# A gated long convolution and its gradients on one core: a 16-point factor on blocks of four channels, and half-partition spectral products in the backward stage

## The chip, the cores and the metric

The kernel runs on one core of one Trainium2 chip. The metric is the device time of one execution in microseconds (us). Four runs of the kernel before gave 566.2 to 569.9 us, with a median of 568.68 us. A second figure, the span in a profile, counts from the first to the last instruction of one profiled execution.

## The reference

Inputs are `A_q`, `A_k`, `A_v` (2048 tokens, 512 channels, bf16), a four-tap filter `shift_k`, a filter `ssm_k` of 2048 taps for each channel, a skip weight `ssm_D`, and the three weights of a gated layer of width 1376. The forward part, cut to what matters:

```python
xn = _layernorm(x)                      # x = A_q
kv = k_shift * v                        # k_shift: k through the four-tap filter
y  = irfft(rfft(pad(kv)) * rfft(pad(ssm_k)))[:, :S] + kv * ssm_D
s  = xn * y
g  = silu((sigmoid(xn @ w_gate) * (xn @ w_up)) @ w_down)
out = x + s * g
```

The kernel returns `out` and the gradients with respect to `A_q`, `A_k`, `A_v`, `shift_k`, `ssm_k`, `ssm_D` and the three weights: ten outputs. The backward part needs the convolution's transpose twice: the gradient `dy` in the spectral domain is multiplied by the conjugate spectrum of the filter (which gives the gradient of `kv`) and by the conjugate spectrum of `kv` (which gives the gradient of `ssm_k`).

## The kernel before

Channels are taken in four groups (`cg`) of 128. The long convolution is a transform of length 4096 made of three matrix steps on TensorE:

- `step1`: for each of 16 token residues `j`, two matmuls with the sine and cosine tables `Cf` (128 x 128 each). The result `Qg` has tokens' frequencies `k` on the partitions.
- `flip`: 32 transposes of 128 x 128 for each group, so that the residue `j` and a block of channels lie on the partitions and `k` lies along the free dimension (`Qf`). A block has eight channels: 16 x 8 = 128 partitions for the real part, and as many for the imaginary part in a second tile.
- `step3`: the factor of 16 points, as a block-diagonal matrix `BD`. A quarter group (`qq`) of 32 channels takes four matmuls of 512 columns (two for the real part, two for the imaginary part) into one PSUM tile of two banks, and one evacuation of 1024 columns.

Then `cmul` makes the product of two spectra on the vector engine (DVE): two operations of 1024 bf16 elements and two of 512. `inv3` is the inverse of `step3`: for each quarter group eight matmuls of 256 columns with the table `R`, and one evacuation. `inv1` is the inverse of `step1` with the tables `Ci`.

The program has three stages.

1. Forward spectral stage, from the start to about 160 us. Four streams of work are interleaved: the gated layer for ten token tiles (`strG`), the filter's spectra (`strK`: transposes of the filter, `step1`, `flip`), the data's spectra (`strV`: the four-tap filter on DVE, `step1`, `flip`), and `strX`, which runs `step3` on both, stores both spectra in DRAM (`KK_d`, lines 956 and 967), multiplies them and transforms back to `y2A`.
2. The gated layer's backward pass (`stepB`, with `z_gen`, `d_gen`, `x_gen`, and `f_gen` for the last tiles), from about 160 to 355 us.
3. Backward spectral stage, from about 360 us to the end: `frontC` runs `step1` and `flip` on the gradient, `backC` the rest for each group, and `dW` makes the three weight gradients (16 matmuls of up to 512 columns for each block), which depend on nothing in the other two streams. `backC` loads both stored spectra of a quarter group with one DMA (`ld_KK`, two buffers), makes two products of 32 channels with `cmul` (lines 1248 and 1249), and two inverses into `B1` and `B2`. At the end of a group come `inv1`, the pair `dks` and `dkv` on DVE, the filter gradient (32 matmuls), the four-tap gradient (16 matmuls and a reduction), and seven DVE operations of 2048 for the gradient of `k`.

No order is left to the hardware. Every operation is recorded (`Rec.add`) with its dependences, and a planner (`Rec.order`, line 337) simulates the five engines with estimated costs (`cost`, line 283, and `dcost`, line 312) and gives out operations in its order of time, on each engine the one that can start first and, among equals, the one recorded first. Each engine's queue then runs strictly in that order. The recorded order comes from `run_streams` (line 497), which interleaves streams by their share of work done. Evacuations of PSUM (`evac`) may go to the scalar engine (ACT) or to DVE; the planner takes DVE when ACT is late by more than a bound (line 404). DMAs are issued on the queue of GpSimd (POOL) or of SyncE (SP), each in order. PSUM tiles of the backward stage have two places of two banks each (`mm2c`), the weight gradients two places of their own (`acc`), and transposes two (`tr`). SBUF is one slab with rings of buffers; a ring's length says how many tiles may be in flight.

All recorded operations carry line 493 in the profile, the line that emits them.

Of the kernel before, what the change touches and what calls it, by code (L numbers as in the profile page):

```python
# [9 lines left out]
ALU = mybir.AluOpType  # L10
# [6 lines left out]
P = 128  # L17
# [20 lines left out]
FBS = [(0, 4), (4, 4), (8, 3)]  # L38

# [129 lines left out]
class Rec:  # L169
# [142 lines left out]
    def dcost(self, alt):  # L312
# [17 lines left out]
        rate = 360e3 if run >= 2048 else 300e3 if run >= 1024 else 250e3 if run >= 512 else 150e3 if run >= 256 else run * 500  # L330
# [6 lines left out]
    def order(self):  # L337
# [53 lines left out]
        while ndone < len(ops):  # L391
            best = None
            for e in self.ENGS:
# [7 lines left out]
                if either and e in ("scalar", "vector"):  # L401
                    o = min(either, key=lambda o: (max(o.ready, free[e]), o.n))
                    s = (max(o.ready, free[e]), o.n, e, 1)
                    late = free["scalar"] - s[0]
                    if e == "scalar" or late > (0.4 if c is None or c[0] > s[0] + 0.6 else 1.6):
                        if c is None or s[:2] < c[:2]:
                            c = s
# [115 lines left out]
def gen_fft_consts(nc, ar, a, b, negpi, Cf, BD, R):  # L523
# [10 lines left out]
    pa = tmp([1], i32)  # L534
    nc.vector.tensor_single_scalar(pa, pi_, 3, ALU.arith_shift_right)
    pe = tmp([1], i32)
    nc.vector.tensor_single_scalar(pe, pi_, 7, ALU.bitwise_and)
    paf = tmp([1], f32)
    nc.vector.tensor_copy(paf, pa)
    pef = tmp([1], f32)  # L540
    nc.vector.tensor_copy(pef, pe)
    cb = tmp([16, 8], f32)
    nc.gpsimd.iota(cb, pattern=[[1, 16], [0, 8]], base=0, channel_multiplier=0, allow_small_or_imprecise_dtypes=True)
    ce = tmp([16, 8], f32)
    nc.gpsimd.iota(ce, pattern=[[0, 16], [1, 8]], base=0, channel_multiplier=0, allow_small_or_imprecise_dtypes=True)
    ab = tmp([16, 8], i32)
    nc.vector.tensor_scalar(ab, cb, paf[:, 0:1], None, ALU.mult)
    mask = tmp([16, 8], f32)
    nc.vector.tensor_scalar(mask, ce, pef[:, 0:1], None, ALU.is_equal)
    ang = tmp([3, 16, 8], i32)  # L550
    nc.vector.tensor_single_scalar(ang[:, 0], ab, 12, ALU.add)
    nc.vector.tensor_single_scalar(ang[:, 1], ab, 8, ALU.add)
    nc.vector.tensor_copy(ang[:, 2], ab)
    nc.vector.tensor_single_scalar(ang, ang, 15, ALU.bitwise_and)
    angf = tmp([3, 16, 8], f32)
# [11 lines left out]
    tri = tmp([3, 16, 8], f32)  # L567
    nc.scalar.activation(tri, angf, ACT.Sin, bias=negpi, scale=2 * math.pi / 16)
    nc.vector.tensor_tensor(tri, tri, mask[:, None, :, :].to_broadcast([P, 3, 16, 8]), ALU.mult)
    nc.vector.tensor_copy(BD, tri.rearrange("p t b e -> p t (b e)"))  # L570
    for c, ci, t in ((0, 0, 0), (0, 1, 1), (1, 0, 2), (1, 1, 0)):
        nc.vector.tensor_scalar(R[:, c, :, :, ci], tri[:, t], SCALE_INV, None, ALU.mult)
# [9 lines left out]
def kernel_impl(ctx, tc, A_q, A_k, A_v, A_shift_k, A_ssm_k, A_ssm_D, B_x, B_w_gate, B_w_up, B_w_down,  # L582
# [8 lines left out]
    KK_d = dram.tile([NG, 4, 2, P, 2, 512], bf16, name="KK_d")  # L591
# [24 lines left out]
    BD = Ring(ar, [3, 128]).ap  # L616
    R = Ring(ar, [2, 16, 8, 2]).ap
# [57 lines left out]
    def f_ln2(i):  # L675
        xj, st = T[i]["xq"], T[i]["st"]
        nc.vector.scalar_tensor_tensor(nmr_all[:, i:i + 1], st[:, 6:7], -1.0, rstd_all[:, i:i + 1], ALU.mult, ALU.mult)
        nc.scalar.activation(xnA[:, i, :], xj, ACT.Identity, bias=nmr_all[:, i:i + 1], scale=rstd_all[:, i:i + 1])
# [55 lines left out]
    QgK_r = Ring(ar, [2, GG, NJ, 8])  # L734
# [5 lines left out]
    QgV_r = Ring(ar, [2, GG, NJ, 8])  # L740
# [76 lines left out]
    QfK_r, QfV_r = Ring(ar, [2, GG, 128], n=2), Ring(ar, [2, GG, 128])  # L817
    KFg_r = Ring(ar, [2, GG, 128])
    Bg_r = Ring(ar, [NJ, GG, 8, 2])
    Xc_r = Ring(ar, [2, 512], n=2)  # L820
    Yc_r = Ring(ar, [2, 512], n=2)
    t2_r = Ring(ar, [2, 512], n=2)
# [10 lines left out]
    def step1(src, Qg):  # L833
        for jb in range(2):
            for c in range(2):
                ps = ps_mm([8, GW], name="ps_q")
                for jj in range(8):
                    j = jb * 8 + jj
                    nc.tensor.matmul(ps[:, jj, :], Cf[:, c, j, :], src(j), start=True, stop=True)
                nc.evac(Qg[:, c, :, jb * 8:(jb + 1) * 8, :].rearrange("p g j e -> p j g e"),  # L840
                         ps[:].rearrange("p j (g e) -> p j g e", e=8), 1024)
                yield 1024

    def flip(Qg, Qf):
        for gb in range(GG // 8):
            for c in range(2):
                pt = ps_tr([8, 128], name="ps_fl")
                for gi in range(8):
                    nc.tensor.transpose(pt[:, gi, :], Qg[:, c, gb * 8 + gi].rearrange("p j e -> p (j e)"), ident)
                nc.evac(Qf[:, c, gb * 8:(gb + 1) * 8, :], pt[:], 1024)  # L850
                yield 1024

    def step3(Qf, qq, dst):
        qre = Qf[:, 0, 4 * qq:4 * qq + 4, :].rearrange("p g k -> p (g k)")
        qim = Qf[:, 1, 4 * qq:4 * qq + 4, :].rearrange("p g k -> p (g k)")
        ps = ps_mm([2, 512], name="ps_x")
        nc.tensor.matmul(ps[:, 0], BD[:, 0, :], qre, start=True, stop=False)
        nc.tensor.matmul(ps[:, 0], BD[:, 1, :], qim, start=False, stop=True)
        nc.tensor.matmul(ps[:, 1], BD[:, 2, :], qre, start=True, stop=False)
        nc.tensor.matmul(ps[:, 1], BD[:, 0, :], qim, start=False, stop=True)  # L860
        nc.evac(dst, ps[:], 1024)
        yield 2048

    def cmul(X, K, out, conj):
        T1, T2 = out, t2_r.next()
        nc.vector.tensor_tensor(out=T1, in0=K, in1=X[:, 0:1, :].to_broadcast([P, 2, 512]), op=ALU.mult)
        nc.vector.tensor_tensor(out=T2, in0=K, in1=X[:, 1:2, :].to_broadcast([P, 2, 512]), op=ALU.mult)
        o0, o1 = (ALU.add, ALU.subtract) if conj else (ALU.subtract, ALU.add)
        nc.vector.tensor_tensor(out=out[:, 0, :], in0=T1[:, 0, :], in1=T2[:, 1, :], op=o0)
        nc.vector.tensor_tensor(out=out[:, 1, :], in0=T2[:, 0, :], in1=T1[:, 1, :], op=o1)  # L870

    def inv3(Y, qq, Bg):
        ps = ps_mm([4, NJ, 16], name="ps_b")
        for gg in range(4):
            for c in range(2):
                nc.tensor.matmul(ps[:, gg].rearrange("p j x -> p (j x)"), Y[:, c, gg * 128:(gg + 1) * 128],
                                 R[:, c].rearrange("p j e c -> p (j e c)"), start=(c == 0), stop=(c == 1))
        nc.evac(Bg[:, :, 4 * qq:4 * qq + 4].rearrange("p j g e c -> p g j (e c)"), ps[:], 1024)
        yield 2048

    def inv1(Bg, dst):
        Bv = Bg.rearrange("p j g e c -> p j (g e) c")
# [64 lines left out]
    def strX():  # L947
        yield from gen_ci()
        for cg in range(NG):
# [4 lines left out]
            for qq in range(4):  # L954
                yield from step3(QfK, qq, KFg[:, :, 4 * qq:4 * qq + 4, :].rearrange("p c g k -> p c (g k)"))
                nc.gpsimd.dma_start(KK_d[cg, qq, 0].rearrange("p c (g k) -> p c g k", k=128), KFg[:, :, 4 * qq:4 * qq + 4, :])
# [6 lines left out]
            for qq in range(5):  # L963
                if qq < 4:
                    Xc = Xc_r.next()
                    yield from step3(QfV, qq, Xc)
                    nc.gpsimd.dma_start(KK_d[cg, qq, 1], Xc)
                    ys[qq] = Yc_r.next()
                    cmul(Xc, KFg[:, :, 4 * qq:4 * qq + 4, :].rearrange("p c g k -> p c (g k)"), ys[qq], False)
                    if qq == 3:  # L970
                        flags.add(("s3V", cg))
                if qq > 0:
# [4 lines left out]
                 (strX(), 4 * 28672 + 4096, 0.2, 1.0)])  # L977
# [447 lines left out]
```

## Time and profile before

| | |
|---|---|
| median of four runs | 568.68 us |
| the profiled execution, its own time | 564.83 us |
| its span | 563.1 us |
| TensorE clock granted | 1.00 throughout |
| matmuls of 128 columns | 3652, 229.9 us busy |
| matmuls of 256 columns | 384, 52.1 us busy |
| matmuls of 512 columns | 1141, 272.1 us busy |
| ACT evacuations of 1024 columns from f32 | 154, mean 1032 ns |
| DVE tensor-tensor, 1024 bf16 elements | 96, mean 684 ns |
| DVE tensor-tensor, 512 bf16 elements | 320, mean 416 ns |
| DVE tensor-tensor, 2048 bf16 elements | 68, mean 1217 ns |
| loads of stored spectra (`KK_d`), POOL queue | 16 of 512 KB, 5.7 us to landing |

How to read it: matmuls are pipelined, so a row's busy time is the union of overlapping instructions, and an instruction's duration is longer than the distance to the next one. "idle before, releaser" says how long an engine stood still before a group and what ended the wait. The chain of waits follows back from the last instruction to what released it. Windows give the busy time of each engine in a stretch, so that a stage can be read alone.

### The profile page before, as it was taken

What the parts mean: (1) busy time and instruction counts of PE and PEld (TensorE: products, weight loads), DVE (VectorE), ACT (ScalarE), POOL (GpSimd) and SP (SyncE); (2) the same over time, 40 slices, a digit from 0 to 9 for tenths busy, and PEclk for the clock granted to TensorE, in tenths of its full rate; (3) what the DMA queues carried; (4) which work ended last, traced back from release to release, by engine and by line L of the source; (5) the groups of instructions that cost most, each with busy time, mean ns of one, the idle gap of its engine ahead of it and who ended that gap; (6) DMA issues with size and microseconds to landing.
All of it is one profiled execution on the core that took longest, in us unless ns stands there. A gap on an engine that the chain in (4) does not pass through costs nothing.

```text
span 563.1 us, 13136 instructions
## 1 busy us (share of the span) xinstructions
PE 536.4 (95%) x5330; PEld 378.5 (67%) x5389; DVE 420.9 (75%) x873; ACT 342.9 (61%) x454; POOL 156.5 (28%) x266
## 2 busy tenths in 40 slices
PE   3999889999989999999999999999999999999996
PEld 2889678898768566776666765656756666565643
DVE  7589899947777998989898999437378487397350
ACT  7989999977986234444344543467758576345421
POOL 3135225303312321312231212313322522331212
PEclk9999999999999999999999999999999999999999
DMA  8899978675522999979979999998487598575433
GB/s 245 239 255 245 308 215 252 215 188 177 173 77 74 214 241 219 278 201 193 238 199 246 247 217 287 291 264 231 139 259 229 177 323 237 160 229 186 152 118 110
DMA packets 127367, 120.34 MB, mean 214 GB/s; under 512 B 74995, under 2 KB 107593, under 8 KB 127306
## 3 DMA queue, kind: packets, MB, share of 16 engines
q1 hardware_dynamic: 109722, 62.84, 46.4%
q0 software_dynamic: 17056, 56.66, 32.4%
q8 instruction: 42, 0.69, 0.5%
q14 instruction: 19, 0.16, 0.1%
q10 hardware_dynamic: 528, 0.00, 0.0%
HBM read 54.23 MB, written 47.55 MB: 181 GB/s over the span
## 4 chain that ended last, share of the span: by engine, by line
PE 72%; issue 9%; ACT 8%; DVE 7%; POOL 2%; DMA 1%; POOLq 0%; ACTq 0%; DVEq 0%
PE psum L493 72%; ACT slab L493 8%; DVE slab L493 7%; POOL out_dram L493 1%; DMA KK_d<-slab 1%; POOL slab L493 0%; POOL KK_d L493 0%; POOLq L1420 0%; POOL ksh_d L493 0%; POOLq L493 0%; ACTq L493 0%; DVEq L493 0%; POOLq L1409 0%
## 5 line engine op out<-in xcount | busy, mean ns | idle before, releaser
L493 PE MATMUL psum<-slab 128*128 128x128 bf16 (+4 forms) x5330 | 536.4, 261 | 21.3 <-ACT slab L493 13.0
L493 PEld LDWEIGHTS <-slab 128*128 128x128 bf16 (+1 forms) x5389 | 378.5, 99 | 178.8 <-issue 13.3
L493 DVE TENSOR_TENSOR slab<-slab 128x512 bf16<-128x512 bf16 (+3 forms) x555 | 291.5, 579 | 37.6 <-ACT slab L493 27.4
L493 ACT CAST slab<-psum 128x1024 bf16<-128x1024 f32 (+3 forms) x242 | 200.1, 857 | 99.3 <-PE psum L493 93.8
L493 ACT COPY slab<-psum 128x1024 bf16<-128x1024 bf16 (+2 forms) x94 | 79.4, 887 | 86.9 <-PE psum L493 86.3
L493 POOL DMA_DIRECT2D out_dram<-slab x75 | 44.6, 596 | 158.7 <-ACT slab L493 83.8
L493 DVE TENSOR_TENSOR slab<-psum,slab 128x512 bf16<-128x512 f32 (+2 forms) x68 | 44.3, 652 | 33.7 <-PE psum L493 24.9
L493 ACT ACTIVATE slab<-slab 128x512 bf16<-128x512 bf16 (+3 forms) x51 | 41.2, 809 | 18.3 <-DVE slab L493 17.9
L493 ACT ACTIVATE slab<-psum 128x512 bf16<-128x512 f32 (+1 forms) x64 | 37.7, 589 | 9.5 <-PE psum L493 8.0
L493 DVE SCALAR_TENSOR_TENSOR slab<-slab 128x1 f32<-128x1 f32 (+3 forms) x64 | 28.0, 437 | 13.8 <-ACT slab L493 12.6
L493 POOL DMA_DIRECT2D KK_d<-slab x32 | 20.0, 628 | 63.3 <-ACT slab L493 54.0
L493 DVE COPY slab<-psum 128x1024 bf16<-128x1024 bf16 (+2 forms) x22 | 14.0, 646 | 20.2 <-PE psum L493 18.7
L493 POOL DMA_DIRECT2D slab<-in_A_q_dram x29 | 16.3, 562 | 39.7 <-DMA out_dram<-slab 31.3
L493 DVE CAST slab<-psum 128x1024 bf16<-128x1024 f32 (+1 forms) x15 | 17.4, 1160 | 9.4 <-PE psum L493 9.2
L493 POOL DMA_DIRECT2D slab<-KK_d x16 | 11.6, 727 | 25.2 <-DVE slab L493 25.1
L493 DVE TENSOR_SCALAR slab<-slab 128x1 f32<-128x1 f32 (+8 forms) x49 | 16.7, 359 | 2.0 <-ACT slab L493 1.8
L493 POOL TENSOR_TENSOR slab<-slab 128x1 f32<-128x1 f32 x16 | 12.7, 796 | 18.7 <-DVE slab L493 18.5
L493 DVE SCALAR_TENSOR_TENSOR slab<-psum,slab 128x512 f32<-128x512 f32 x16 | 10.9, 684 | 6.7 <-PE psum L493 6.7
L493 POOL DMA_DIRECT2D slab<-in_grad_out_dram x16 | 8.7, 541 | 22.1 <-DMA out_dram<-slab 15.4
L493 POOL DMA_DIRECT2D slab<-slab x8 | 4.5, 567 | 26.6 <-issue 17.3
L493 DVE BATCH_NORM_STATS2 slab<-slab 128x6 f32<-128x512 bf16 x16 | 10.8, 683 | 0.0
L493 POOL DMA_DIRECT2D slab<-in_A_k_dram x12 | 10.1, 844 | 2.2 <-PE psum L493 1.7
(22 smaller groups left out, 44.4 us busy)
## 6 DMA issues: line engine op xcount, KB each, us to landing
KK_d<-slab POOLq DMA_DIRECT2D x32, 256.0 KB, 3.3
slab<-KK_d POOLq DMA_DIRECT2D x16, 512.0 KB, 5.7
out_dram<-slab POOLq DMA_DIRECT2D x58, 128.0 KB, 4.2
hS_d<-slab SPq DMA_DIRECT2D x16, 352.0 KB, 3.0
dgS_d<-slab SPq DMA_DIRECT2D x16, 352.0 KB, 5.0
duS_d<-slab SPq DMA_DIRECT2D x16, 352.0 KB, 4.8
slab<-hS_d SPq DMA_DIRECT2D x8, 512.0 KB, 5.0
slab<-dgS_d SPq DMA_DIRECT2D x8, 512.0 KB, 5.7
```

The lines of the kernel that those rows point to most:

```text
L493: getattr(getattr(self.nc, eng), meth)(*[place(v) for v in a], **{x: place(v) for x, v in k.items()})
```

## The change

A block has four channels instead of eight, and the real and imaginary parts share one tile: partition index = part (2) x residue (16) x channel (4). The constants have nine sections, each a (offset, factor) pair of angles, where the factor depends on the half of the partitions.

- `step3` takes a table index. One result of 1024 columns (a quarter group of 32 channels, both parts) takes two matmuls of 512 columns. `X_RI` gives (real, imaginary) in the two halves, `X_IR` the two exchanged, `X_IN` (imaginary, minus real).
- The filter's spectrum takes `X_RI` alone. The data's spectrum in the forward stage takes `X_RI` and `X_IR`, each with an evacuation of its own.
- The forward product is two full operations of 1024 and no sum: the sum over the parts is made by `inv3`, with two terms (`R_A`, `R_B`), 16 matmuls of 128 columns for a quarter group.
- In the backward stage `step3` makes `Xr` (`X_RI`) and `Xi` (`X_IN`). Each of the two products is four operations of 1024 on 64 partitions, two of which write the half that they don't read, and one full sum. `K` is overwritten. `inv3` then has one term (`R_W`), 8 matmuls of 128 columns for each product.
- Stored spectra are laid out so that a quarter group is 2 x 1024 for each partition. Their load goes to the SP queue, with four buffers and three quarters ahead instead of two. `Qf` has one buffer instead of two; `frontC` waits for the group before, between `step1` and `flip`.
- The layer norm's last step may go to ACT or DVE. The planner's DMA rates and its rule for evacuations change.

```diff
+GQ = GW // 4
+HALF = (0, 1)
+SECS = [(12, -4), (0, 12), (4, -4), (12, -8), (8, -8), (0, 0), (12, 0), (12, 4), (8, 4)]
+BDSEC = [(0, 1), (1, 0), (1, 2)]
+RSEC = [(3, 4), (5, 6), (7, 8)]
...
-        rate = 360e3 if run >= 2048 else 300e3 if run >= 1024 else 250e3 if run >= 512 else 150e3 if run >= 256 else run * 500
+        rate = 340e3 if run >= 2048 else 290e3 if run >= 1024 else 250e3 if run >= 512 else 150e3 if run >= 256 else run * 500
...
-                    late = free["scalar"] - s[0]
-                    if e == "scalar" or late > (0.4 if c is None or c[0] > s[0] + 0.6 else 1.6):
+                    late = free["scalar"] + self.cost(o.alts[0])[0] - s[0] - self.cost(o.alts[1])[0]
+                    if e == "scalar" or late > (0.3 if c is None or c[0] > s[0] + 0.6 else 1.5):
...
+    for n, (off, d) in enumerate(SECS):
+        if d:
+            nc.vector.tensor_scalar(ang[:, n], ab, dc[d][:, 0:1], float(off), ALU.add, ALU.add)
+        else:
+            nc.vector.tensor_single_scalar(ang[:, n], ab, float(off), ALU.add)
...
-        nc.scalar.activation(xnA[:, i, :], xj, ACT.Identity, bias=nmr_all[:, i:i + 1], scale=rstd_all[:, i:i + 1])
+        nc.add([("scalar", "activation", (xnA[:, i, :], xj, ACT.Identity), dict(bias=b, scale=r)),
+                ("vector", "tensor_scalar", (xnA[:, i, :], xj, r, b, ALU.mult, ALU.add), {})])
...
-                    nc.tensor.transpose(pt[:, gi, :], Qg[:, c, gb * 8 + gi].rearrange("p j e -> p (j e)"), ident)
+                nc.tensor.transpose(pt[:, gi, :], Qg.rearrange("p c j e g -> p (c j e) g")[:, :, g], ident)
...
+    def step3(Qf, qq, which, dst):
         ps = ps_mm([2, 512], name="ps_x")
-        nc.tensor.matmul(ps[:, 0], BD[:, 0, :], qre, start=True, stop=False)
-        nc.tensor.matmul(ps[:, 0], BD[:, 1, :], qim, start=False, stop=True)
-        nc.tensor.matmul(ps[:, 1], BD[:, 2, :], qre, start=True, stop=False)
-        nc.tensor.matmul(ps[:, 1], BD[:, 0, :], qim, start=False, stop=True)
+        lhs = BD[:, which].rearrange("p c j e -> p (c j e)")
+        for h in range(2):
+            nc.tensor.matmul(ps[:, h], lhs, Qf[:, 8 * qq + 4 * h:8 * qq + 4 * h + 4, :].rearrange("p g k -> p (g k)"),
+                             start=True, stop=True)
...
+    def inv3(terms, qq, Bg):
+        ps = ps_mm([8, NJ, 8], name="ps_b")
+        for g in range(8):
+            for n, (Y, r) in enumerate(terms):
+                nc.tensor.matmul(ps[:, g].rearrange("p j x -> p (j x)"), Y[:, g * 128:(g + 1) * 128],
+                                 R[:, r].rearrange("p j e c -> p (j e c)"), start=(n == 0), stop=(n == len(terms) - 1))
...
+                    yield from step3(QfV, qq, X_RI, Xc)
+                    nc.gpsimd.dma_start(KK_d[cg, qq, :, 1], Xc)
+                    nc.vector.tensor_tensor(Y, Xc, KFg[:, qq], ALU.mult)
+                    yield from step3(QfV, qq, X_IR, Xs)
+                    nc.vector.tensor_tensor(Xs, Xs, KFg[:, qq], ALU.mult)
+                    ys[qq] = ((Y, R_A), (Xs, R_B))
...
-            nc.gpsimd.dma_start(KK, KK_d[n // 4, n % 4].rearrange("t p c x -> p t c x"))
+            nc.sync.dma_start(KK, KK_d[n // 4, n % 4])
...
-            while cg > 1 and ("s3C", cg - 2) not in flags:
-                yield 0
             Qg = Qg_r.next()
             yield from step1(lambda j: y2A[:, j, cg * GW:(cg + 1) * GW], Qg)
+            while cg > 0 and ("s3C", cg - 1) not in flags:
+                yield 0
...
-                    cmul(Xc, KK[:, 0], Y1, True)
-                    cmul(Xc, KK[:, 1], Y2, True)
+                    lo, hi = slice(0, 64), slice(64, P)
+                    for t in range(2):
+                        K, T2 = KK[:, t], ys[qq][1][:, t]
+                        if t in HALF:
+                            nc.vector.tensor_tensor(T2[lo], K[lo], Xr[lo], ALU.mult)
+                            nc.vector.tensor_tensor(T2[hi], K[lo], Xi[lo], ALU.mult)
+                            nc.vector.tensor_tensor(K[lo], K[hi], Xr[hi], ALU.mult)
+                            nc.vector.tensor_tensor(K[hi], K[hi], Xi[hi], ALU.mult)
+                            nc.vector.tensor_tensor(T2, T2, K, ALU.add)
...
-                    yield from inv3(Y1, qq - 1, B1)
-                    ld_KK(cg * 4 + qq + 1)
-                    yield from inv3(Y2, qq - 1, B2)
+                    for t, B in ((0, B1), (1, B2)):
+                        yield from inv3(((T2[:, t], R_W),), qq - 1, B)
+                    ld_KK(cg * 4 + qq + 3)
...
-    KK_r = Ring(ar, [2, 2, 512], n=2)
-    Qf_r = Ring(ar, [2, GG, 128], n=2)
+    KK_r = Ring(ar, [2, 1024], n=4)
+    Qf_r = Ring(ar, [GQ, 128])
...
+    Xr_r, Xi_r, T2_r = Ring(ar, [1024], n=2), Ring(ar, [1024], n=2), Ring(ar, [2, 1024], n=2)
```

## The prediction

> **What bounds the kernel now.** I read the page first: busy shares, then the 40 slices, then the windows by stage, then the vector engine's timeline in the last stage.
>
> ```profile
> PE 536.4 (95%) x5330; PEld 378.5 (67%) x5389; DVE 420.9 (75%) x873; ACT 342.9 (61%) x454; POOL 156.5 (28%) x266
> ...
> PE 72%; issue 9%; ACT 8%; DVE 7%; POOL 2%; DMA 1%; POOLq 0%; ACTq 0%; DVEq 0%
> ```
>
> TensorE is the bound on average, and 72% of the chain of waits lies on it. But the change touches two stages only, so the windows decide (columns: the stretch and its length, busy us of PE, PEld, DVE, ACT and POOL with instructions, granted clock, DMA share, GB/s):
>
> ```profile
> 20.00:60.00 40.00, 38.66 (x617) 35.63 (x618) 34.05 (x60) 36.01 (x49) 16.14 (x26) 1.00 0.90 239
> 60.00:100.00 40.00, 35.19 (x466) 29.61 (x468) 37.70 (x65) 38.44 (x49) 15.55 (x25) 1.00 0.88 253
> ...
> 200.00:240.00 40.00, 39.84 (x423) 27.96 (x425) 36.61 (x96) 18.90 (x33) 10.74 (x19) 1.00 1.02 241
> ...
> 400.00:440.00 40.00, 39.73 (x337) 26.62 (x340) 28.15 (x45) 27.64 (x31) 11.29 (x18) 1.00 0.69 218
> 440.00:480.00 40.00, 39.68 (x310) 24.99 (x314) 27.70 (x45) 25.86 (x29) 14.77 (x21) 1.00 0.74 230
> ```
>
> In the forward spectral stage (13 to about 160 us) TensorE, ACT and DVE are all near full. In the backward spectral stage (from about 366) TensorE never pauses, and DVE and ACT have 30% each to spare. The DVE timeline there:
>
> ```profile
> 376.47 7.71 DVE L493 TENSOR_TENSOR slab<-slab 128x1024 bf16<-128x1024 bf16 x16 [1.67 <-ACT slab L493]
> ...
> 402.88 2.48 DVE L493 TENSOR_TENSOR slab<-slab 128x2048 bf16<-128x2048 bf16 x2 [7.67 <-ACT slab L493]
> ...
> 514.98 3.96 DVE L493 TENSOR_TENSOR slab<-slab 128x1024 bf16<-128x1024 bf16 x8 [1.28 <-DMA slab<-KK_d]
> 525.42 2.48 DVE L493 TENSOR_TENSOR slab<-slab 128x2048 bf16<-128x2048 bf16 x2 [6.47 <-ACT slab L493]
> ...
> 537.96 7.50 DVE L493 TENSOR_TENSOR slab<-slab 128x2048 bf16<-128x2048 bf16 x6
> ```
>
> The first spectral products start at 376.5, the pair `dks`/`dkv` of the first channel group comes at 402.9 and that of the last at 525.4, so a group takes 40.9 us. The last product ends at 518.9 and the last DVE operation at 545.5: a tail of 26.5 us, mostly latency. The 1 MB store of `out_2` follows (7.5 us to landing by the list of DMA issues, about 9 with its issue), so this branch would end near 554.5; the weight gradients on TensorE end the kernel after it. The branch has some 9 us of slack.
>
> Rates. In the forms list a tensor-tensor of 1024 lasts 684 ns and one of 512 417. The 16 in 7.71 us are eight of each; the durations sum to 8.81, so neighbours overlap by 73 ns: start to start 0.611 and 0.344, and one complex product takes 1.93. One of 2048 takes 1.22. The last full weight-gradient blocks are evacuated at 541.35, 544.81 and 548.26: 3.46 us for 16 matmuls of 512 columns, 216 ns each, so 108 for 256 columns. A stretch of 176 matmuls in 10.13 us gives 57.6 ns for 128 columns.
>
> [...] The 64 existing filter transposes step by 32 bytes, yet the 3652 matmuls of 128 columns average 220 ns, latency included[...].
>
> **The change part by part.**
>
> *Start.* Nine sections of constants instead of three: some 4 more 128x1 operations at 0.14 us, 6 more angle operations at 0.2, larger masks, then more copies. About 2 us of DVE ahead of the first sine (7.28), more behind it. TensorE is half idle there (11.46 of 20 us). Between 0 and +2; I take +1.
>
> *Forward, TensorE.* Filter spectra: 16 quarter groups x 2 fewer matmuls of 512 = 32 x 0.216 = -6.9. The data spectra keep their 4. The inverse becomes 16 of 128 instead of 8 of 256: 16 x (0.92-0.86) = +0.9. Sum -6.0.
>
> *Forward, ACT and DVE.* 16 more evacuations, 1.03 each: +16.5. Products: 1.93 becomes 2 x 0.611, 16 times: -11. The normalisation of 13 tiles may go from ACT (0.86) to DVE (estimate 0.2 from the 1408-element tensor_scalar at 0.54): -8. Net about -3 over the two engines. ACT is 90 to 96% busy in 20 to 100, so TensorE's 6 us come off only in part: bounds -6 and +3, I take -3.5. Start and forward: -2.5. The stage between (160 to 355) keeps its work.
>
> *Flips.* 384 transposes read every 32nd element. Bounds: 0, or a doubled pace (50 ns, 19 us); I take 0.
>
> *Backward, TensorE.* step3 keeps 4 x 512. The inverses: 16 x 256 become 16 x 128 per quarter group: 16 x (1.73-0.92) = -13.0. The weight gradients come forward into that room.
>
> *Backward, ACT.* 16 more evacuations, 1.03: from 69% to about 79%. Hidden.
>
> *The planner.* Its transfer rates fall by 3 to 6%, and the choice of an evacuation's engine now compares finishing times, which favours DVE for bf16 tiles (0.69 there, 1.06 on ACT) and ACT for f32 ones (1.22, 1.03). In the backward stage DVE has 4 bf16 evacuations now; four more would cost it 2.8 us, four fewer give as much. I take 0.
>
> *Backward, DVE.* Per quarter group, two products at 1.93 (3.86) become 10 operations of 1024, eight on 64 partitions[...]. Below: 10 x 0.611 = 6.1. [...] I take the held order: four of five at 0.684, 6.7 us. A group then costs 26.8 for products and 12.4 for the rest (9 x 1.22, 2 x 0.69), 39.2 against 27.8 now. TensorE's 40.9 us per group shrinks by 3.3, and by more where fewer gradients are interleaved. So the spare 30% is gone, and DVE sets the group. From the first product: 4 x 39.2 - 12.4 (the last group's rest lies in the tail) = 144.4. Stage 200 to 240 has DVE at 91.5% busy while not the bound; as the bound I take 96%: 150.4. The tail loses a little, as fewer gradients stand between: 24. End: 376.5 - 2.5 + 150.4 + 24 + 9 = 557.4.
>
> *Waits and queues.* An inverse waiting for the sum holds TensorE's queue: step3 of the next quarter and gradients stand behind it. The gradients are the cover as long as the written order puts them before the wait; its estimate for 1024 elements (0.603 in `cost`) is right for back-to-back operations but 10 us short over 128 held ones, which is what TensorE may wait. The spectra's load moves from POOL to SP, two quarters earlier, into 4 buffers: 16 issues of 0.73 us leave POOL, and the DVE waits on that load (5.2 us) go. On SP they stand among gradient loads which wait for their buffer; three quarters ahead is some 20 us of cover. `Qf` has one buffer: the next flip waits for the group's last step3, covered by its remaining products.
>
> *Sum.* TensorE's branch: 563.1 - 2.5 - 13.0 = 547.6 plus up to 10. DVE's branch: 557.4. The later counts: -5.7. The profiled execution took 564.83 (span 563.1 and 1.7 around it), so 559.1; it lies 3.9 under the median shown, so 563.0.
>
> **Rivals.**
>
> 1. TensorE keeps all it saves. Half operations overlap: 160 x 0.611 + 37.2 = 135.0, at 96% 140.6, end 547.6, equal to TensorE's branch: -15.5, 553.2. For it: DVE's 30% idle now[...].
> 2. Slower: DVE overruns in the backward stage. It decides from 152.5 us of DVE work (0.72 us per operation at 96%), or from 9% idle at my price: 374 + 158.9 + 33 = 565.9. With 14% idle, as the 6 to 8 us gaps at the group ends suggest if next-group products don't fill them: 374 + 167.9 + 33 = 574.9, +11.8: 580.5. [...] For it: those gaps; against: the four load buffers and two of `T2` allow half a group ahead.
> 3. DVE's branch ends just where TensorE's does now, and ACT eats the forward gain: 568.
>
> **How the numbers follow.** Forecast 0.35, rival 1 0.24, rival 2 0.27, rival 3 0.14. Faster by over 0.5% (about what a measurement can tell from no change): 0.28 of the forecast and rival 1, 0.52. Slower: rival 2 and 0.04 of rival 3, 0.31. Same: the rest, 0.17. Range 551 to 579: the PE bound with some forward gain below, rival 2 with 13% idle above. Both signs hold much, so the forecast's own range: 558 to 567.
>
> **What would show it.** DVE in 400 to 480 at 37 us of 40 or more, where it now has 28, and half operations starting 0.68 us apart; TensorE's waits naming DVE, above 5 us in all, from 366 on; the last DVE operation within 10 us of the end; `dks` pairs 39 to 42 us apart. Forward: the stage ends 2 to 5 us earlier. Wrong if TensorE ends at full occupancy with DVE under 85% in the backward stage (rival 1), if half operations last about 1.2 us, or if flips pace above 60 ns.

## The result and the profile after

| | before | after |
|---|---|---|
| median of all runs, us | 569.26 (63 runs) | 570.87 (44 runs) |
| ratio, 95% interval | 1 | 1.0041 [1.0026, 1.0055] |
| span of the profiled execution, us | 563.1 | 569.7 |
| last matmul of the weight gradients ends, us | 557.7 | 565.3 |
| last DVE operation ends, us | 545.5 | 553.3 |

By the prediction's own sums (6.0 us forward, 13.0 backward) the change takes some 19 us of matmuls out of the kernel, and yet it is 0.4% slower: a small difference, but the interval leaves out 1. The forecast was 5.7 us faster. The profiled execution of the kernel before took 564.83 us, 4.4 less than its median, and that of the changed kernel 571.5, 0.6 more than its own, so the two traces lie 6.7 us apart where the medians lie 1.6 apart. The page of the changed kernel, first its busy times and then the chain of waits:

```profile
PE 527.9 (93%) x5426; PEld 373.4 (66%) x5485; DVE 466.4 (82%) x908; ACT 359.7 (63%) x469; POOL 140.2 (25%) x250
...
PEclk9999999999999999999999999999999999999699
...
PE 44%; DVE 28%; ACT 11%; issue 11%; DMA 4%; POOL 2%; POOLq 0%; DVEq 0%; ACTq 0%
```

The chain was 72% TensorE and 7% DVE; now it is 44% and 28%. One slice of the 40 (527 to 541 us) has a granted clock of 6 tenths; the profiled execution of the kernel before has none such. All 44 executions of the changed kernel have a mean clock of 0.990 to 0.994, so this is not a matter of the one that was profiled. The windows by stage say where TensorE's room opens (columns as before: PE, PEld, DVE, ACT, POOL, clock, DMA share, GB/s):

```profile
20.00:60.00 40.00, 37.38 (x598) 35.41 (x599) 33.76 (x59) 34.00 (x43) 13.29 (x23) 1.00 0.77 199
60.00:100.00 40.00, 35.34 (x498) 30.71 (x503) 36.41 (x59) 38.96 (x49) 14.26 (x26) 1.00 0.89 276
...
400.00:440.00 40.00, 38.99 (x325) 24.17 (x329) 33.19 (x46) 31.47 (x37) 8.88 (x15) 1.00 0.68 221
440.00:480.00 40.00, 39.07 (x322) 23.79 (x326) 37.55 (x55) 28.28 (x33) 10.62 (x16) 1.00 0.72 233
480.00:520.00 40.00, 36.00 (x267) 20.88 (x269) 39.03 (x50) 22.80 (x28) 11.01 (x19) 1.00 0.63 191
520.00:570.00 50.00, 39.24 (x255) 23.28 (x255) 23.87 (x33) 14.57 (x20) 9.28 (x15) 0.90 0.36 110
```

From 400 to 480 TensorE is at 39 of 40 (39.7 before), with DVE risen from 28 to 33 and 38. From 480 on DVE has no room left (39.03 of 40) and TensorE loses 4 us in one window, more in the next. The same window of the kernel before, and the stretch from 360 to 560 us, first before and then after:

```profile
480.00:520.00 40.00, 39.79 (x260) 23.51 (x262) 28.15 (x45) 16.95 (x21) 11.93 (x20) 1.00 0.61 198
...
360.00:560.00 200.00, 196.41 (x1437) 121.08 (x1460) 115.98 (x192) 109.59 (x129) 56.34 (x88) 1.00 0.69 208
...
360.00:560.00 200.00, 186.77 (x1409) 111.32 (x1432) 161.46 (x225) 120.75 (x141) 44.64 (x72) 0.97 0.67 203
```

In the changed kernel TensorE's matmuls stood still for 13.2 us from 360 us to the last of them. Before it was 1.3: of the 3.6 us in the row, 2.3 lie behind its last matmul. The waits from 360 us to the end name what TensorE stood for (engine, what it waited for, us in total, times, longest), first before and then after:

```profile
PEld L493 <- DVE slab L493: 2.0, 9, 0.3
...
PEld L502 <- DVE slab L502: 16.7, 19, 4.0
PE psum L502 <- DVE slab L502: 8.8, 10, 3.5
```

A weight load and the matmul that uses it can stand in the same hole, and a weight load can wait while matmuls run, so these rows are not lost time to be added up; the loss is the 13.2 us above. The rows say whom TensorE waited for, and I go by the weight loads' row from here on: 16.7 us for DVE, where the kernel before had 2.0 (and no row for its matmuls). All operations have line 502 now, since they are recorded by a helper; it was 493. The timeline of TensorE in the last backward group (start, length, operation and count, idle time before it and what ended it) shows what was missing:

```profile
494.82 15.62 PE L502 MATMUL psum<-slab 128*128 128x128 bf16 x113
511.64 7.31 PE L502 MATMUL psum<-slab 128*128 128x128 bf16 x38 [1.20 <-DVE slab L502]
519.52 3.52 PE L502 MATMUL psum<-slab 128*128 128x128 bf16 x26 [0.56 <-DVE slab L502]
526.58 1.03 PE L502 MATMUL psum<-slab 128*128 128x128 bf16 x8 [3.54 <-DVE slab L502]
528.62 1.03 PE L502 MATMUL psum<-slab 128*128 128x128 bf16 x8 [1.00 <-DVE slab L502]
```

The two stretches of 8 matmuls in 1.03 us are inverses and nothing else: each waits for its product's sum, and no gradient stands between two of them. From 523.0 to 534.1 us the trace has no gradient matmul (512 columns) at all. From 526.2 the granted clock is half for 10.2 us, then full again; by windows of 10 us:

```profile
520.00:530.00 10.00, 4.98 (x37) 2.87 (x35) 9.62 (x15) 3.83 (x5) 0.98 (x2) 0.81 0.44 131
530.00:540.00 10.00, 9.02 (x82) 7.40 (x84) 5.13 (x6) 5.13 (x6) 1.28 (x2) 0.68 0.23 63
```

Why were there no gradients? The load queue on SP answers, by its waits from 490 to 545 us, first before and then after:

```profile
SPq L493 <- PE psum L493: 39.2, 10, 21.2
SPq L493 <- DVE slab L493: 4.8, 1, 4.8
...
SPq L502 <- DVE slab L502: 36.1, 5, 13.4
SPq L502 <- ACT slab L502: 11.4, 1, 11.4
SPq L502 <- PE psum L502: 9.2, 4, 6.6
```

In the kernel before, the loads waited for TensorE. In the changed one the last gradient job but one loads its data into the space of the spectra's four buffers, and each of its four loads waits until a product has read the buffer for the last time: they were issued at 504.0, 519.5, 526.6 and 531.5, the last landed at 535.3. So the cover for the inverses (the independent matmuls that fill their waits) waited for DVE itself. From 523 us until DVE was through with the products (531.5), TensorE had only inverses, and those waited for DVE too; the gradients left then ran behind it, to 565.3.

### The profile page after: what moved, and what is told of

It is laid out like the page before. It is cut to its first block, busy times and chain, and to the rows that moved or that the text cites. A ratio compares the mean times of both kernels' runs of the same rounds, so it can differ in the third digit from the quotient of the medians.

```text
span 569.7 us, 13401 instructions
## 1 busy us (share of the span) xinstructions
PE 527.9 (93%) x5426; PEld 373.4 (66%) x5485; DVE 466.4 (82%) x908; ACT 359.7 (63%) x469; POOL 140.2 (25%) x250
## 4 chain that ended last, share of the span: by engine, by line
PE 44%; DVE 28%; ACT 11%; issue 11%; DMA 4%; POOL 2%; POOLq 0%; DVEq 0%; ACTq 0%
PE psum L502 44%; DVE slab L502 28%; ACT slab L502 11%; DMA slab<-in_A_k_dram 2%; POOL out_dram L502 1%; DMA ksh_d<-slab 1%; POOL slab L502 1%; DMA slab<-dgS_d 1%; DMA slab<-in_A_shift_k_dram 0%; ACT L502 0%; POOLq L1434 0%; DVEq L502 0%; ACTq L502 0%; POOLq L502 0%
## 5 line engine op out<-in xcount | busy, mean ns | idle before, releaser
L502 PE MATMUL psum<-slab 128*128 128x128 bf16 (+3 forms) x5426 | 527.9, 258 | 37.5 <-ACT slab L502 16.4
L502 PEld LDWEIGHTS <-slab 128*128 128x128 bf16 (+1 forms) x5485 | 373.4, 103 | 191.6 <-issue 23.1
L502 DVE TENSOR_TENSOR slab<-slab 128x512 bf16<-128x512 bf16 (+5 forms) x555 | 324.3, 626 | 19.3 <-ACT slab L502 12.5
L502 ACT CAST slab<-psum 128x1024 bf16<-128x1024 f32 (+3 forms) x271 | 224.7, 878 | 90.4 <-PE psum L502 74.6
L502 ACT COPY slab<-psum 128x1024 bf16<-128x1024 bf16 (+1 forms) x84 | 71.8, 873 | 86.1 <-PE psum L502 85.8
L502 ACT ACTIVATE slab<-slab 128x512 bf16<-128x512 bf16 (+3 forms) x47 | 37.4, 800 | 17.4 <-DVE slab L502 16.8
L502 DVE COPY slab<-psum 128x1024 bf16<-128x1024 bf16 (+2 forms) x32 | 19.7, 623 | 15.7 <-PE psum L502 14.5
L502 DVE CAST slab<-psum 128x1024 bf16<-128x1024 f32 (+1 forms) x18 | 21.5, 1193 | 6.9 <-PE psum L502 5.3
L502 DVE TENSOR_SCALAR slab<-slab 128x1 f32<-128x1 f32 (+8 forms) x68 | 19.5, 321 | 3.4 <-ACT slab L502 2.0
L502 DVE SCALAR_TENSOR_TENSOR slab<-psum,slab 128x512 f32<-128x512 f32 x16 | 10.9, 684 | 7.0 <-PE psum L502 6.8
L502 POOL MEMSET slab<- 1x384 bf16 (+4 forms) x14 | 5.7, 417 | 13.8 <-DVE slab L502 12.2
```

What stands on the lines that cost most here:

```text
L502: getattr(getattr(self.nc, eng), meth)(*[place(v) for v in a], **{x: place(v) for x, v in k.items()})
```

## The experiments

A ratio stands against the kernel before, timed in alternation, with its 95% interval. The question came in two halves: what starves TensorE behind 480 us, and what became of the 6 us that the forward stage should have given.

### Which part of the change costs what

Theory A at this point: the order written by the planner takes a half operation for 0.603 us, the profile shows 0.65 to 0.72 from one start to the next, so the inverses are placed too early in TensorE's queue. **e1** gives the planner that price and changes nothing else:

```diff
+            if meth == "tensor_tensor" and out.shape[0] == 64:
+                c += 0.1
```

> Only the planner's estimate changes: a tensor-tensor on 64 partitions costs 0.1 us more, so the written order knows what the trace of the changed kernel shows[...]. Theory A (the DVE is nearly full in the backward stage and TensorE, written for a faster DVE, waits with gradient matmuls queued behind it): TensorE's waits for DVE from 360 us on fall from about 24 us (matmuls and weight loads) to under 12, the last DVE operation stays near 553, the span falls by 4 to 8 us, ratio to before 0.992 to 0.998. Theory B (the amount of DVE work alone sets the end): last DVE operation and span as in the changed kernel, ratio 1.002 to 1.006. Theory C (more evacuations on ACT and the shared PSUM places hold TensorE): the waits for ACT stay and the span falls by less than 2 us.

Measured: 565.9 us, 0.9945 [0.9924, 0.9966]. The time fell as theory A had it, and the last DVE operation came 3.8 us earlier (549.5). But the waits did not fall as it said: those of the weight loads for DVE only from 16.7 to 11.4 us (from 25.5 to 19.8 with the matmuls' row, where under 12 was expected), and one of some 7 us remains:

```profile
PEld L504 <- DVE slab L504: 11.4, 8, 7.2
...
PE psum L504 <- DVE slab L504: 8.4, 4, 7.0
```

These rows are the waits of e1 from 360 us on; 7.2 and 7.0 are the same hole (516.5 to 523.6), seen by a weight load and by its matmul. With the price known, operations that come 0.1 us late each hardly make a hole of 7; there was no other work ahead of this inverse in TensorE's queue. So I took it that something besides the price was missing.

**e2** does the half-partition way for one of the two products of a quarter group; the other keeps two full products and an inverse of two terms, as before. **e3** does it for neither. All else of the change stays.

```diff
-HALF = (0, 1)
+HALF = (1,)
...
+                        terms = ((T2[:, t], R_W),) if t in HALF else ((KK[:, t], R_C), (T2[:, t], R_B))
```

> Only the second product is made in half-partition operations; the first is two full operations, and the inverse sums its two terms (16 matmuls of 128 instead of 8). Theory A: DVE loses 16 x (5 x 0.67 - 1.2) = 34 us in the backward stage and is at 80% there, TensorE gains 16 x 8 x 0.058 = 7.4 us of work but its waits for DVE go back to under 6 us; span 552 to 557, ratio 0.980 to 0.990. Theory C (ACT and PSUM places): evacuations are as many as in the changed kernel, so the waits stay and the ratio is 1.00 to 1.015, as TensorE has more to do.

> Both backward products are two full operations, both inverses sum two terms; no operation on 64 partitions is left. Theory A: DVE loses another 34 us and TensorE gains another 7.4; TensorE is full again from 360 us, ratio 0.99 to 1.00, slower than e2_one_half by 4 to 8 us. Theory C: ratio 1.01 or more.

Measured: e2 568.08 us, 1.0006 [0.9987, 1.0024]; e3 567.85, 0.9997 [0.9977, 1.0017]. The expectation for e2 missed by over 1%. e3 says more than its time does: its waits for DVE from 360 us are

```profile
PEld L502 <- DVE slab L502: 0.4, 2, 0.2
```

so the half-partition way, with the load on DVE that comes with it, is the origin of all the backward waiting. Theory C of the expectations falls with this too: e3 has as many evacuations as the changed kernel, and TensorE waits neither for DVE nor for ACT in that stretch. But e3 also keeps the forward saving, by the prediction 6 us of matmuls, and is no faster than the kernel before: the forward saving is lost by itself, in the forward stage. The windows up to 160 us show it as idle time of TensorE: 15.5 us in the kernel before, 21.5 in the changed one, 21.7 in e3.

### Where the forward 6 us went

Three changes to the forward part. **e4** puts back the planner's former transfer rates, its former choice of an evacuation's engine and the former place of the normalisation. **e5** records the large table of constants ahead of the nine sections instead of behind them, with the same operations. **e6** leaves out the exchanged spectrum in the forward stage: its matmuls still run, into the same PSUM tile, but there is one evacuation where there were two, and the second product reads the first one's copy.

> The changed kernel with the planner's former transfer rates, its former rule for the engine of an evacuation, and the layer norm's last step on ACT alone. Theory D (the new rule loses the forward stage's gain): the first spectral products of the backward stage start 4 to 6 us earlier than at 378.0 and the ratio falls to 0.993 to 0.998. Otherwise (start and full ACT and DVE lose it): start of those products within 2 us of 378 or later, ratio 1.000 to 1.010.

> The changed kernel with the nine sections of constants recorded behind the sine and cosine tables instead of ahead of them; nothing else differs. If the new small DVE operations ahead of the second half of the tables delay the start, TensorE's lost time at 20 us falls from 15.5 to about 13 us (before: 12.9), the backward stage's first product starts 2 to 3 us before 378.0, ratio 0.997 to 1.001. If the start is hidden, the first product stays within 1 us of 378.

> Leaves out the exchanged spectrum of the data in the forward stage: its two matmuls still run, but into the same PSUM tile as the plain one, which is evacuated once; the second product reads the plain spectrum. So TensorE's work is that of the changed kernel and 16 evacuations (16.5 us of ACT) and 16 uses of a PSUM place are gone. If these eat the forward stage's saving on TensorE, the backward stage's first product starts 4 to 6 us earlier than at 378.0. If it is the order or the start that eats it, the start moves by less than 2 us.

Measured: e4 568.55, 1.0002 [0.9982, 1.0022]; e5 579.86, 1.0209 [1.0133, 1.0285]; e6, a single execution, 567.0. The time of the first spectral product of the backward stage shows what the earlier stages took: 376.5 before, 378.0 in the changed kernel, 375.3 in e4, 374.1 in e6. So the 16 added evacuations eat 3.9 of the 6 us by e6 (4 to 6 were expected), and the planner's new rates and rules, with the place of the normalisation, perhaps 2 more (e4 came 2.7 us earlier, less than the 4 to 6 of its theory D). e5 is a miss with a lesson: moving a few recorded instructions, with no work added, made the kernel 2% slower. Its first spectral product comes at 382.6, 4.6 us later than in the changed kernel, and about 3 us more are lost behind that. Nothing but the recorded order differs, and so the order that the planner wrote. A difference of 2 or 3 us between two single orders is therefore weak evidence about a cause, and the split of the forward loss stays rough.

One part of it no experiment took out. The flips now read every 32nd element of `Qg`. The weight loads of one flip, in the kernel before and in the changed one (ns: least, median, most):

```profile
L493 PEld LDWEIGHTS <-slab x8: 98/98/98, 362.5 to 362.9; 128*128 128x128 bf16 x8
...
L502 PEld LDWEIGHTS <-slab x7: 150/153/158, 363.7 to 364.1; 128*128 128x128 bf16 x7
```

Most of that is hidden, but the flips' matmuls now start 62 to 64 ns apart (55.9 before). At some 7 ns each, the 384 flips cost 2.7 us by this estimate, 1.8 of them in the forward stage.

### Price and rules together

**e8** takes one half product, the price, the constants of e5 and the old rules of e4; **e9** is that without the constants; **e10** has no half product and the old rules; **e11** has both half products, price and old rules; **e12** is e9 without the old rules. (The run e7 is the kernel of e2 once more, 568.3 us in a single execution; one half product with the price is e12.)

> One product in half-partition operations, the planner told of their price, constants behind the tables, former planner rules. Each took its part by itself: start -2.5 us, former rules -2, price -3 to -5 against e2_one_half (1.0006). If the parts add, the ratio is 0.984 to 0.992 and TensorE loses under 9 us from 360 on. If the backward stage waits for something else than DVE's price, it still loses 14 there and the ratio is 0.993 or more.

> One product in half-partition operations, the planner told of their price, former planner rules, constants where the change has them: e8_combined without the moved constants, which lost time in e5_consts_last. If the forward stage is the one of e4_old_rule (35 us lost by TensorE at 160) and the backward stage the one of e8_combined (10 lost from 360 on), the ratio is 0.988 to 0.994. If forward and backward losses come with any new order at random, it is within 0.996 to 1.004.

> No half-partition operation, former planner rules: TensorE has 7 us more to do than in e9_one_price_rule and loses 8 us from 360 on, as in e3_no_half. Ratio 0.993 to 0.998, between e9_one_price_rule and e3_no_half.

> Both products in half-partition operations, price and former rules. DVE stays at 37 to 39 us of 40 in the backward stage, so its branch (last operation near 545 to 550) holds the end: ratio 0.990 to 0.998, not below e9_one_price_rule by more than 0.3%.

> e2_one_half with the planner told of the price of half-partition operations, and the changed kernel's own planner rules: it splits the step from e2_one_half (1.0006) to e9_one_price_rule (0.9886) into price and rules. If the price is the larger part, TensorE loses 8 to 10 us from 360 on instead of 14 and the ratio is 0.991 to 0.995; if the rules are, 0.996 to 1.000.

| | half products | price | old rules | us | ratio |
|---|---|---|---|---|---|
| e2 | 1 | no | no | 568.08 | 1.0006 [0.9987, 1.0024] |
| e12 | 1 | yes | no | 562.53 | 0.9889 [0.9845, 0.9933] |
| e9 | 1 | yes | yes | 561.46 | 0.9886 [0.9838, 0.9934] |
| e8 | 1 | yes | yes, constants moved | 565.79 | 0.9980 [0.9954, 1.0006] |
| e1 | 2 | yes | no | 565.90 | 0.9945 [0.9924, 0.9966] |
| e11 | 2 | yes | yes | 564.08 | 0.9922 [0.9897, 0.9948] |
| e10 | 0 | no | yes | 566.39 | 0.9977 [0.9951, 1.0003] |

The price is worth 1.2% with one half product and 1.0% with two. The old rules are worth nothing that the intervals can tell once the price is in (e9 against e12, e11 against e1) or with no half product (e10 against e3); with two half products and no price they are worth 0.4% (e4 against the changed kernel, 1.0002 and 1.0041, whose intervals do not meet). e8 is a miss (0.984 to 0.992 expected): it carries the moved constants of e5, and e9, which leaves them out, came as expected. With one half product and the price, the weight loads' waits for DVE from 360 us are down from 10.9 us in e2 to 4.1:

```profile
PEld L504 <- DVE slab L504: 4.1, 12, 0.9
```

(e12's waits from 360 us.) So with DVE less loaded the price alone is enough. With two half products it isn't, which left the cover itself as the suspect.

### The cover

The gradients are interleaved with the backward stage by shares: the stage's generator is given the weight that it will yield, 4 x 38912 + 4096 = 159744, and the point of the gradients at which it should end, 0.66. Before the change it really yielded 4 x 44544 + 4096 = 182272, so with its start at -0.05 it ended at -0.05 + 0.71 x 182272/159744 = 0.76 of the gradients. After it yields 4 x 36352 + 4096 = 149504, as the inverses have half the columns, and ends at 0.61. The change leaves the weight and the end as they stand. Theory E, as the expectations call it: too large a part of the gradients is put behind the stage instead of inside it, and what there is of them inside is bound to buffers that come free late. **e13** restores the share, **e14** restores it and gives the price too, **e15** does that with one half product.

```diff
-                        (gated(backC(), "back"), 4 * 38912 + 4096, -0.05, 0.66)], until=lambda: "back" in flags)
+                        (gated(backC(), "back"), 4 * 38912 + 4096, -0.05, 0.815)], until=lambda: "back" in flags)
```

> The changed kernel with backC's end in the interleaving at 0.815 instead of 0.66, so that its last work is written where 76% of the gradients are done, as before the change; nothing else. Theory E (the filler has no data): no gradient load waits for the DVE any more, TensorE's lost time from 500 to 540 falls from 13 us to under 5 and its clock is not halved there, ratio 0.986 to 0.995. Theory A alone (price of half operations): TensorE's lost time from 360 on stays above 20 us, ratio 0.999 to 1.006.

> Share as in e13_share and the planner told of the price. If both causes are real and add, TensorE loses under 10 us from 360 on and the time is 2 to 6 us below e13_share; if the share is the whole cause, within 2 us of e13_share; if the price is, near e1_price (0.9945).

> e12_one_price with the new share. There TensorE lost only 10 us from 360 on, so little is left: within 0.4% of e12_one_price (0.9889); slower if the backward stage's tail comes out last.

| | half products | price | share | us | ratio |
|---|---|---|---|---|---|
| changed kernel | 2 | no | 0.61 | 570.87 | 1.0041 [1.0026, 1.0055] |
| e1 | 2 | yes | 0.61 | 565.90 | 0.9945 [0.9924, 0.9966] |
| e13 | 2 | no | 0.76 | 562.24 | 0.9895 [0.9854, 0.9935] |
| e14 | 2 | yes | 0.76 | 559.00 | 0.9834 [0.9795, 0.9873] |
| e15 | 1 | yes | 0.76 | 563.17 | 0.9904 [0.9875, 0.9933] |

Against the changed kernel the price gives 1.0%, the share 1.5%, both 2.1%. e14 is the best version run: 1.7% under the kernel before. Its executions (558.25 to 560.09 us) and those of e13 (561.46 to 564.6) don't overlap, so the price adds something to the share too. In e13 the half clock near 526 is gone, but the waits for DVE, many and short, are:

```profile
PEld L502 <- DVE slab L502: 13.0, 19, 2.3
```

(e13's waits from 360 to 565 us; the longest is 2.3, where it was 4.0.) Its windows say where the gain lies:

```profile
480.00:520.00 40.00, 35.89 (x272) 20.91 (x270) 39.06 (x50) 22.32 (x27) 10.87 (x18) 1.00 0.65 209
...
520.00:530.00 10.00, 9.66 (x87) 6.00 (x86) 8.85 (x14) 4.38 (x6) 1.08 (x2) 1.00 0.61 170
```

From 480 to 520 TensorE is no better off than in the changed kernel (36.00); from 520 to 530 it has 9.66 of 10, where it had 4.98. So the share removes the long hole at the end, and the price the small misplacements before it. e14 has neither. Its waits in the same stretch:

```profile
PEld L504 <- DVE slab L504: 3.7, 9, 0.8
```

Its windows, with the columns as above:

```profile
440.00:480.00 40.00, 39.15 (x323) 24.21 (x322) 37.61 (x53) 28.44 (x34) 10.60 (x16) 1.00 0.75 238
480.00:520.00 40.00, 39.61 (x291) 22.41 (x289) 38.62 (x52) 23.70 (x28) 11.66 (x20) 1.00 0.75 226
```

And the timeline of TensorE, for the last backward group and what follows:

```profile
494.72 20.32 PE L504 MATMUL psum<-slab 128*128 128x512 bf16 x123
515.34 32.42 PE L504 MATMUL psum<-slab 128*128 128x128 bf16 x234 [0.30 <-DVE slab L504]
```

DVE is as full as in the changed kernel (37.61 and 38.62 against 37.55 and 39.03), and TensorE has 39.61 in the window where that kernel had 36.00. From 494.7 to 547.8 TensorE pauses once, for 0.30 us. From 490 to 545 us no load of the gradients waits for DVE any more, and the last has landed at 519.2. So it was not the amount of DVE work that made the change slow, but where the gradients and the inverses stood in the order. Nor was it the rest of the change: e14 keeps the one `Qf` buffer, the loads on SP and the 16 more evacuations.

With one half product the share gives nothing on top of the price (e15 0.9904 against e12 0.9889): DVE isn't full there and the cover wasn't missing.

## Why the prediction was wrong

**Right.** An operation on half the partitions was priced like one on all of them. No trace of the kernel before has one, so that was an estimate, and it holds. In the forms list from 354 us on:

```profile
L502 DVE TENSOR_TENSOR slab<-slab 64x1024 bf16<-64x1024 bf16 x128 | 84.6, 684 | 4.0 <-ACT slab L502 1.5
```

684 ns, like the 687 of the 128-partition ones. The held order is there too. By it the prediction means that four of a product's five operations begin only when the one before is done, and so cost their full 0.684 us instead of 0.611; nothing in the trace of before shows it, it was an estimate as well. The chain of waits in the last group has such operations one by one (start, length, engine; the partitions are not in the trace, I take them from the order in the program):

```profile
515.18 0.69 DVE slab L502
515.89 0.69 DVE slab L502
516.61 0.69 DVE slab L502
517.33 0.70 DVE slab L502
```

They start 0.71 to 0.72 apart. In the first group, starts are 0.60 to 0.61 apart where an operation's input and output begin in the same half of the partitions as those of the one before, and 0.71 to 0.72 where one of them begins in the other half; 0.65 on average. In the second case an operation starts 0.03 us after the one before has ended, in the first 0.07 to 0.09 us ahead of that end. I had 0.61 and 0.684. The `dks` pairs come 42 us apart on the average (39 to 42 forecast), though single groups take 37 to 47. DVE has 37.6 and 39.0 of 40 from 440 to 520, but 33.2 from 400 to 440, where I asked for 37. The waits on the spectra's load are gone.

**The DVE branch, late by 5 us but rightly built.** First product at 378.0 (forecast 374.0), end of the last at 531.5 (524.4), end of the last DVE operation at 553.3 (548.4):

```profile
377.99 26.05 DVE L502 TENSOR_TENSOR slab<-slab 64x1024 bf16<-64x1024 bf16 x40
...
503.24 28.21 DVE L502 TENSOR_TENSOR slab<-slab 128x1024 bf16<-128x1024 bf16 x36
...
545.77 7.53 DVE L502 TENSOR_TENSOR slab<-slab 128x2048 bf16<-128x2048 bf16 x6 [1.08 <-DMA slab<-slab]
```

(the DVE timeline). Of the 7 us at the last product, 4 are the start and forward term, 3 the groups: DVE was busy 142.4 of the 153.5 us between, 93% where I took 96. The tail gives 2 back. With the last operation at 553.3 and 9 for the store, this branch ends near 562, not at 569.7. In e14, where TensorE no longer stands, this branch does set the end: TensorE and DVE both end at 547.8, the store of `out_2` lands at 555.1, and the span is 556.6, against the 557.4 that I had for this branch.

**Start and forward, a wrong size.** The term was -2.5 and measured +1.5 (376.5 to 378.0). I let ACT take 2.5 of the 6 us of matmuls, and 1 for the start. The evacuations cost 3.9 (e6, one order), ACT was at 38.96 of 40, TensorE was busy 9.2 of the first 20 us instead of 11.5, and the slower flips took 1.8 by the estimate above. These do not add up exactly, but together they took all of the 6 and more.

**Flips, a term put at nothing.** I took strided reads to be free, because all 3652 matmuls of 128 columns average 220 ns. The 64 transposes that step through memory are too few to show in that mean; their weight loads, read alone, take some 150 ns in the kernel before as well, and the others 98. The sign that I gave, a pace above 60 ns, came: 62 to 64. It is a small term, 2.7 us in all.

**The step that failed** is the sum: "TensorE's branch: 563.1 - 2.5 - 13.0 = 547.6 plus up to 10", and under it the sentence "The gradients are the cover as long as the written order puts them before the wait". The branch measured 569.7: 22.1 above the 547.6. Of these 4.0 are the forward term; 18.1 are what came on in the backward stage, where I allowed 10. TensorE stood still there for 13.2 us instead of 1.3, nearly all of it for DVE, which is 11.9; and 10.2 us at half clock, in which matmuls of 128 columns start 107 ns apart instead of 56, are up to 5.1 more. (Some 5 of the 22 us come from the executions that happened to be profiled: by the medians the forecast missed by 7.3.) I took the misplacement from the planner's estimate (10 us short over 128 held operations), and that part wasn't too small: with the price alone e1 is 5.0 us faster than the changed kernel. What I didn't do is count the cover: how many gradients the interleaving by share would put inside a stage that yields 18% less weight, and into whose buffers their data would be loaded. That was to be read in the kernel: the 38912 in `run_streams` is not what `backC` yields, before or after. With the share back and nothing else (e13) the kernel takes 562.24, 8.6 us less than the changed one, and with the price as well 559.0. That 562.24 is almost the forecast number is chance.

**Rivals.** Rival 3's number (568) is nearest, and ACT eating the forward gain was its half of the truth; its other half, DVE's branch ending where TensorE did before, is nearly so (562 and 563). But neither of the two set the end. Rival 2 had the right place (the backward stage, for want of DVE) but a wrong cause: it let DVE idle for 14% at the group ends, and DVE idled for 7%, the most of it in the first group. Rival 1's 553.2 wasn't reached by any version; e14, at 559.0, is the nearest.

**Left open.** Why each forward order is some us better or worse; e5 shows the size of this, not its reason. Whether the holes in TensorE's work brought the half clock. And whether fewer evacuations in the forward stage on top of e14 would bring its 4 us: not tried.

## What to carry to other kernels

When work leaves an engine whose gaps are filled by interleaved independent work, recompute the shares of the interleaving: the filler's place was set for the old amount, and what was 0.76 became 0.61 without a line about it in the diff. Count the cover in the stage where the new wait falls, with the time at which its data can be loaded, and ask whose release that load waits for; if it is the engine that is now late, the cover vanishes just when it is needed. An order written from estimates needs the price of the new operation form, here 0.1 us each, before its effect can be judged.

## What the runs showed of the hardware

A DVE tensor-tensor of 1024 bf16 elements on 64 partitions lasts 684 ns, as on 128 (687). Those that write the half they don't read take no longer (677 to 687 ns in the first group of the changed kernel, by the order in the program; the others on 64 partitions 673 to 692). Where the half changes from one operation to the next, starts are 0.71 to 0.72 us apart instead of 0.60 to 0.61: about 0.11 us for each, the overlap with the one before.

A transpose on TensorE whose input steps by 32 bf16 elements (64 bytes) loads it as weights in 153 ns instead of 98, and such transposes follow one another in 62 to 64 ns instead of 56.

In the changed kernel TensorE was at half clock for 10.2 us from 526.2, after windows in which it was busy 8.18 of 10 us (510 to 520) and 4.98 of 10 (520 to 530); in e1 for 10.2 us from 518.9, which lies inside its hole of 7 us. e13 and e14, with at least 9.4 of 10 us from 510 to 540, don't show it there. So in these two traces a hole came with a loss beyond its own length. That the hole brings it is not shown. e14 was granted 0.96 of the clock from 60 to 100 us, with TensorE busy 37.29 of these 40 us and 36.43 of the 40 before them. And e2 and e7 are one kernel, whose 23 executions had mean clocks from 0.996 to 1.000.
